# Scores and exponentials of the next batch moved ahead of product 1, and the softmax sums interleaved with the sums of r

## The chip, the cores and the metric

The kernel runs on one core of a Trainium2 chip. The metric is the device time of one launch in microseconds (us), the median of several executions. Before the change it is 144.81 us (three runs, 144.69 to 145.2). All times below come from one profiled execution of the same program, which took 144.88 us, and are counted from the start of its span.

## The reference

There are 8 batches. In each batch 8 heads hold x (512 x 64) and state (32 x 64). The first part is a cross attention in both directions, the second a two-branch layer with a maximum:

```python
scores  = scale * x @ state.T;  a  = softmax(scores)      # over the 32 states
xread   = a @ state                                        # 512 rows a head
scores2 = scale * state @ x.T;  a2 = softmax(scores2)      # over the 512 rows
sread   = a2 @ x                                           # 32 rows a head
rows    = concatenate([xread, sread])                      # 544 a batch, 512 wide
g       = maximum(rows @ w1, rows @ w2)                    # 1024 wide
out     = g @ w_out                                        # 4352 x 512, float32
```

The kernel uses max(h1, h2) = h2 + relu(h1 - h2), so that only one matrix, w1 - w2, needs a relu and the term h2 @ w_out goes through the product w2 @ w_out. It also puts the state through these matrices first, so that the attention weights a are multiplied with "state times weights".

## The kernel before

**Setup and pipeline.** A list of tokens at the head of the file (ORDER) writes out, instruction by instruction, the loading of the weights and the work of batches 0 and 1. Then a loop over b = 2 to 6 runs; each pass finishes batch b and prepares batch n = b + 1. A tail finishes batch 7 and the 256 sread rows. Nothing reorders the work: each engine executes its instructions in the order in which the code issues them, and engines wait for one another by semaphores.

**The pass of the loop.** The names that are used below:

- **l1** (line 375): eight banks f0 to f7 of PSUM get "state weights times a of b"; the relus go in turn to ACT (f0, f2, f4, f6, line 368) and DVE (f1, f3, f5, f7, line 370) and give r of the batch.
- **Seven products instead of eight** (line 426): r times w_out for 512 rows by 512 columns is made from seven quarter products, in Winograd's form of Strassen's scheme. Each is 8 matmuls of 256 columns. Three PSUM accumulators pX, pY and pZ take them. Their left sides are quarters of r (rq) or sums of those, st[0] to st[3], which DVE makes (**r_sum** 0 to 3, line 402, two bf16 inputs of 128 x 1024). r_sum 1 reads st[0], r_sum 3 reads st[1].
- **keep** 0, 1, 2 (line 102 on ACT) copies a partial accumulator away so that it can be added to a later one; **put** (line 402 or 104 on DVE, one on ACT) writes a quarter of the output; **opened** (line 432) adds the h2 term.
- For batch n: **sc_mm** (line 264, two halves of 8 small matmuls with xt, x transposed, as weights), **sc_ev** (line 272, an exponential on ACT for each half), **red** (lines 276 and 277, on DVE the sum over 32 states and its reciprocal, for each half), **mul** (line 280, on POOL the division of each half), **at_dma** (line 285, a transposing DMA of a on SP's queue), **sw_mm** (line 352, state times weights, three pairs of banks), **sw_ev** (their copies, mostly on ACT), **sr_mm** (line 304) and **sr_tr** (line 336) for sread.
- POOL further casts x of later batches (line 106) and makes differences of weights (line 402).

**Banks.** pX, pY and pZ have a bank each. The other five are used in a fixed ring: l1 takes eight turns of it, then sc_mm two, sw_mm five (one of its six banks is pY's), sr_mm one and sr_tr one or two. So the two banks of sc_mm are those of f3 and f4, and the last pair of sw_mm takes the banks of sc_mm.

**Buffers.** e, a and xt have two buffers each, used in turn by even and odd batches; the results of at_dma and the state weights sw have three.

Of the kernel before, what the change touches and what calls it, by code (L numbers as in the profile page):

```python
# [57 lines left out]
def kernel(  # L58
# [32 lines left out]
    def bank(ring="r", dtype=F32):  # L91
        if isinstance(ring, int):
            i = ring
        else:
            r = rings[ring]
            i = r[turn[ring] % len(r)]
            turn[ring] += 1
        return banks[i] if dtype == F32 else banks[i].bitcast(BF16)
# [142 lines left out]
    def xt_dma(b):  # L241
        nc.sync.dma_start_transpose(out=xt_s[b % 2].rearrange("p c k t -> p (c k) t"),
                                    in_=xb_s[b % 2].rearrange("p c m -> p (c m)"))
# [14 lines left out]
    def sc_mm(b, hh, ring="r"):  # L258
        p = bank(ring)
        pv = p.rearrange("p (c g i n) -> p c i g n", c=NC, g=2, i=2)  # L260
        for c in range(NC):
            for kk in range(2):
                k = 2 * hh + kk
                nc.tensor.matmul(pv[:, c, kk], xt_s[b % 2][:, c, k, :], sbd[:, b, k, :],  # L264
                                 start=(c == 0 and kk == 0), stop=(c == NC - 1 and kk == 1))
        return p

    def e_view(t, hh):
        return t.rearrange("p g c i n -> p (g c) i n")[:, :, 2 * hh:2 * hh + 2, :]

    def sc_ev(p, b, hh):
        nc.scalar.activation(out=e_view(e_s[b % 2], hh).rearrange("p (g c) i n -> p g c (i n)", g=2),  # L272
                             in_=p.rearrange("p (c g m) -> p g c m", c=NC, g=2), func=ACTF.Exp, scale=scale)

    def red(b, hh):
        nc.vector.tensor_reduce(es_all[:, b, hh], e_view(e_s[b % 2], hh), axis=AXX, op=ALU.add)  # L276
        nc.vector.reciprocal(er_s[b % 2][:, hh], es_all[:, b, hh])  # L277

    def mul(b, hh, eng):
        (nc.gpsimd if eng == "P" else nc.vector).tensor_mul(  # L280
            e_view(a_s[b % 2], hh), e_view(e_s[b % 2], hh),
            er_s[b % 2][:, hh].unsqueeze(3).to_broadcast([128, 2 * NC, 2, Ns]))

    def at_dma(b):
        nc.sync.dma_start_transpose(out=at_s[b % 3].rearrange("p g c t -> p (g c) t"),
                                    in_=a_s[b % 2].rearrange("p g c i n -> p (g c i n)"))
# [59 lines left out]
    def sw_mm(b, lo, hi, rA="r", rB="r"):  # L346
        pg = [bank(rA), bank(rB)]
        n = hi - lo
        for i in range(4):
            for g in range(2):  # L350
                rhs = wd[64 * g:64 * g + 64, i, lo:hi] if hi <= FF else wwo[64 * g:64 * g + 64, i, lo - FF:hi - FF]
                nc.tensor.matmul(pg[g][32 * i:32 * i + 32, 0:n],  # L352
                                 sbd[64 * g:64 * g + 64, b, i, 32 * g:32 * g + 32], rhs, start=True, stop=True)
        return pg

    def sw_ev(pg, b, lo, hi, g, eng):
        copy(eng, sw_s[b % 3][:, g, lo:hi], pg[g][:, 0:hi - lo])
# [14 lines left out]
    def l1_mm(b, f, ring="r"):  # L372
        p = bank(ring)
        for g in range(2):
            nc.tensor.matmul(p, sw_s[b % 3][:, g, f * 128:(f + 1) * 128], at_s[b % 3][:, g].rearrange("p c t -> p (c t)"),  # L375
                             start=(g == 0), stop=(g == 1))
        return p

    def l1_ev(p, b, f, eng=None):
        relu(r_s[b % 2][:, f, :], p, eng)  # L380
# [20 lines left out]
    def add(eng, o, i0, i1, op=ALU.add):  # L401
        (nc.gpsimd if eng == "P" else nc.vector).tensor_tensor(o, i0, i1, op=op)  # L402

    def wq(j, k):
        return wo[:, 4 * j:4 * j + 4, 256 * k:256 * k + 256]

    def rq(b, i, j):
        return r_s[b % 2][:, 4 * j:4 * j + 4, 256 * i:256 * i + 256]
# [5 lines left out]
    def r_sum(b, k, eng):  # L414
        a, c, op = ((rq(b, 1, 0), rq(b, 1, 1), ALU.add), (st[:, 0], rq(b, 0, 0), ALU.subtract),
                    (rq(b, 0, 0), rq(b, 1, 0), ALU.subtract), (rq(b, 0, 1), st[:, 1], ALU.subtract))[k]
        add(eng, st[:, k], a, c, op)
# [5 lines left out]
    def product(pv, lhs, rhs, first=False, cc=(0, 1)):  # L423
        for c in cc:
            for f in range(4):
                nc.tensor.matmul(pv[c], lhs[:, f, 128 * c:128 * c + 128], rhs[:, f, :],  # L426
                                 start=first and f == 0 and (c == 0 or pv.split), stop=False, skip_group_check=True)

    def opened(b, pv, i, rhs, cc=(0, 1)):
        for c in cc:  # L430
            for g in range(2):
                nc.tensor.matmul(pv[c], at_s[b % 3][:, g, 2 * i + c, :], rhs[:, g, :], start=False, stop=False,  # L432
                                 skip_group_check=True)
# [12 lines left out]
    def keep(k, pv, eng):  # L446
        if pv.split:
            for c in range(2):
                copy(eng[c], part[:, k, 256 * c:256 * c + 256], pv[c])
        else:  # L450
            copy(eng, part[:, k], pv.p[0])
# [11 lines left out]
    def so_half(b, k):  # L463
        return sw_s[b % 3][:, :, FF + 256 * k:FF + 256 * k + 256]

    def store(b, c0=0, c1=NC, lo=0, hi=DM, eng=None):
        dst = out[b * L:b * L + S].rearrange("(p c) n -> p c n", c=NC)
        (eng or nc.sync).dma_start(out=dst[:, c0:c1, lo:hi], in_=ob(b)[:, c0:c1, lo:hi])
# [265 lines left out]
    for b in range(2, B - 1):  # L734
        n = b + 1
        if b + 2 < B and b != 3:
            xt_dma(b + 2)
        for f in range(NF):
            l1_ev(l1_mm(b, f), b, f)
        pX, pY, pZ = Pair(BX), Pair(BY), Pair(BZ)  # L740
        product(pX, rq(b, 0, 0), wq(0, 0), True)
        keep(0, pX, "A")
        r_sum(b, 0, "V")
        r_sum(b, 1, "V")
        pp = [sc_mm(n, hh) for hh in range(2)]
        for hh in range(2):
            sc_ev(pp[hh], n, hh)
        product(pZ, rq(b, 0, 1), wq(1, 0), True)
        opened(b, pZ, 0, so_half(b, 0))
        pg = [sw_mm(n, 512 * z, 512 * z + 512, BY if z == 0 else "r") for z in range(3)]  # L750
        sw_ev(pg[0], n, 0, 512, 0, "A")
        sw_ev(pg[0], n, 0, 512, 1, "A")
        for hh in range(2):
            red(n, hh)
            mul(n, hh, "P")
        at_dma(n)
        if b == 3:
            xt_dma(b + 2)
        if b == 2:
            store(1)  # L760
        if b + 4 < B - 1:
            for g in range(2):
                load_x(b + 4, g)
        elif b + 4 < B:
            load_x(b + 4, 0, n=H)
        r_sum(b, 2, "V")
        product(pX, st[:, 1], wt[:, 1])
        sw_ev(pg[1], n, 512, 1024, 0, "A")
        keep(1, pX, "A")
        put(b, 0, 0, pZ, 0)  # L770
        sw_ev(pg[1], n, 512, 1024, 1, "V")
        sw_ev(pg[2], n, 1024, 1536, 0, "A")
        product(pY, st[:, 0], wt[:, 0], True)
        keep(2, pY, "A")
        r_sum(b, 3, "V")
        sw_ev(pg[2], n, 1024, 1536, 1, "A")
        if b + 2 < B:
            for k in range(4):
                cast_e(b + 2, k, "P")
        difference(n, "P")  # L780
        if b + 3 < B:
            for g in range(2):
                cast_b(b + 3, g, "P")
        if b < 6:
            v_sum(b - 2, "P")
        product(pX, st[:, 2], wt[:, 2])
        opened(b, pX, 1, so_half(b, 1))
        p = sr_mm(n, "r")
        put(b, 1, 1, pX, 2)
        sr_ev(p, n)  # L790
        if b < 4:
            sr_ev(srd[:, b - 2], b - 2)
        if n == B - 1:
            check_sums()
        product(pY, st[:, 3], wq(1, 1))
        opened(b, pY, 0, so_half(b, 1))
        put(b, 0, 1, pY, 1)
        product(pX, rq(b, 1, 1), wt[:, 3])
        opened(b, pX, 1, dif[:, b % 2])
        if b < 4:  # L800
            sr_cp(sr_tr(b - 2, "r"), b - 2, "A")
        sr_cp(sr_tr(n, "r"), n, "A")
        put(b, 1, 0, pX, None, "A")
        if n == B - 1:
            for k in range(4):
                m_sum(k, aq, sst, "P")
            p = bank("r")
            nc.tensor.matmul(p[:, 0:1], full, bad, start=True, stop=True)
            nc.vector.tensor_copy(flag[0:1, :], p[0:1, 0:1])
        store(b)  # L810
# [91 lines left out]
```

## Time and profile before

| What | Value |
|---|---|
| median of 3 runs | 144.81 us |
| the profiled execution | 144.88 us, its span 143.1 us |
| PE matmul busy | 134.7 us, 94% of the span |
| DVE / ACT / POOL busy | 108.3 / 86.9 / 72.1 us |
| the five passes of the loop | 52.72 to 119.47 us, 66.75 us |
| mean granted TensorE clock | 0.996 |

The view of stretches gives for each pass the busy time of every engine. The timeline lists an engine's instructions with start and duration; several of one kind in a row are one row with their count. The bracket behind a row is the idle time ahead of it and what ended it. The chain of waits follows the work that ended last backward; a row of it gives a start, a duration, an engine and a line.

### The profile page before, as it was taken

To read this page: it belongs to the slowest core of one execution; us is meant where nothing else is said; L and a number is where in the kernel's file an instruction comes from. 1 tells how busy PE (TensorE), PEld (TensorE's weight loads), DVE (VectorE), ACT (ScalarE), POOL (GpSimd) and SP (SyncE) were. 2 spreads that over 40 slices of the span, in tenths; PEclk is the share of its full clock that TensorE was granted. 3 is DMA by queue.
4 is the path that set the end of the run, shared out by engine and by line. 5 is a ranking of instruction groups with operands and counts; after the bars stand their busy time and mean duration, and the time that the engine had idled before them with its cause. 6 is when DMAs were issued, how large, how long until landed. Compare 5 with 4: busy or idle time off the path is not lost.

```text
span 143.1 us, 3680 instructions
## 1 busy us (share of the span) xinstructions
PE 134.7 (94%) x1448; PEld 95.4 (67%) x1458; DVE 108.3 (76%) x197; ACT 86.9 (61%) x168; POOL 72.1 (50%) x99
## 2 busy tenths in 40 slices
PE   6889989999999999999999999999999999999980
PEld 2467725456787776786778477747876786788860
DVE  3488959868999938997899799669948997847420
ACT  4367589895689535855682769086726855753220
POOL 4147326099009993399269908971990464200000
PEclk9999999999999999999999999999999999999998
DMA  3999999945997979949995999759137042502073
GB/s 112 342 366 392 384 386 386 343 83 93 196 343 230 286 180 249 236 42 293 242 386 109 212 355 195 160 213 211 35 65 293 2 58 82 234 5 73 9 248 119
DMA packets 36452, 29.50 MB, mean 206 GB/s; under 512 B 22608, under 2 KB 32336, under 8 KB 35536
## 3 DMA queue, kind: packets, MB, share of 16 engines
q1 hardware_dynamic: 36160, 29.10, 70.8%
q8 instruction: 12, 0.20, 0.6%
q10 hardware_dynamic: 272, 0.13, 0.3%
q14 instruction: 8, 0.07, 0.1%
HBM read 15.20 MB, written 8.91 MB: 169 GB/s over the span
## 4 chain that ended last, share of the span: by engine, by line
PE 83%; DMA 11%; ACT 1%; issue 1%; DVE 0%; SPq 0%; DVEq 0%
PE bank L426 36%; PE bank L375 19%; PE bank L432 10%; DMA big<-in_moe_w_out_dram 8%; PE bank L352 5%; DMA big<-in_x_dram 4%; PE bank L606 3%; PE bank L473 2%; PE bank L515 2%; PE bank L264 2%; PE bank L304 2%; PE bank L513 1%; ACT wo L102 1%; PE bank L548 1%; PE bank L336 0%
## 5 line engine op out<-in xcount | busy, mean ns | idle before, releaser
L102 ACT COPY big<-bank 128x512 f32<-128x512 f32 (+2 forms) x40 | 21.9, 551 | 16.6 <-PE bank L426 8.4
L280 POOL TENSOR_TENSOR a<-e,er 128x512 bf16<-128x512 bf16 x14 | 16.7, 1209 | 29.5 <-ACT e L272 18.0
L370 DVE TENSOR_SCALAR r<-bank 128x512 bf16<-128x512 f32 x32 | 21.9, 690 | 11.7 <-PE bank L375 10.6
L375 PE MATMUL bank<-at,sw 128*128 128x512 bf16 x120 | 29.1, 379 | 0.6 <-DVE sw L104 0.2
L426 PEld LDWEIGHTS <-big 128*128 128x128 bf16 x256 | 23.9, 98 | 6.3 <-DVE er L277 2.1
L426 PE MATMUL bank<-big,big 128*128 128x256 bf16 x192 | 23.1, 273 | 0.1
L102 ACT CAST sw<-bank 128x512 bf16<-128x512 f32 x36 | 20.1, 608 | 3.2 <-PE bank L352 3.2
L375 PEld LDWEIGHTS <-sw 128*128 128x128 bf16 x128 | 12.2, 98 | 13.5 <-ACT sw L102 0.5
L368 ACT ACTIVATE r<-bank 128x512 bf16<-128x512 f32 x32 | 18.3, 597 | 4.9 <-PE bank L375 4.7
L426 PEld LDWEIGHTS <-r 128*128 128x128 bf16 x192 | 18.2, 98 | 3.8 <-issue 0.5
L402 DVE TENSOR_TENSOR big<-bank,big 128x512 f32<-128x512 f32 (+1 forms) x25 | 16.4, 660 | 5.4 <-PE bank L432 5.4
L106 POOL CAST xe<-big 128x512 bf16<-128x512 f32 x23 | 16.5, 749 | 6.1 <-DMA big<-in_x_dram 6.1
L426 PE MATMUL bank<-wo,r 128*128 128x256 bf16 x128 | 16.3, 273 | 0.0
L102 ACT COPY sread_t<-bank 128x128 bf16<-128x128 bf16 x8 | 3.2, 472 | 18.7 <-PE bank L336 15.5
L106 POOL CAST xb<-big 128x1024 bf16<-128x1024 f32 x12 | 12.2, 1035 | 4.7 <-DMA big<-in_x_dram 4.7
L432 PE MATMUL bank<-sw,at 128*128 128x256 bf16 x96 | 14.4, 273 | 0.0
L432 PEld LDWEIGHTS <-at 128*128 128x128 bf16 x128 | 12.5, 98 | 1.7
L402 DVE TENSOR_TENSOR big<-r 128x1024 bf16<-128x1024 bf16 x16 | 12.6, 788 | 0.6
L276 DVE TENSOR_REDUCE sums<-e 128x16 f32<-128x512 bf16 x16 | 10.6, 660 | 0.3 <-ACT e L272 0.2
L272 ACT ACTIVATE e<-bank 128x512 bf16<-128x512 f32 x16 | 8.9, 601 | 1.3 <-PE bank L264 1.3
L402 POOL TENSOR_TENSOR big<-sw 128x512 bf16<-128x512 bf16 x8 | 9.2, 1151 | 0.9 <-POOL a L280 0.9
L104 DVE CAST sw<-bank 128x512 bf16<-128x512 f32 x12 | 7.9, 679 | 0.6 <-PE bank L352 0.6
(100 smaller groups left out, 188.7 us busy)
## 6 DMA issues: line engine op xcount, KB each, us to landing
big<-in_x_dram SPq DMA_DIRECT2D x14, 512.0 KB, 6.2
out_dram<-big SPq DMA_DIRECT2D x7, 1024.0 KB, 5.3
big<-in_moe_w_dram SPq DMA_DIRECT2D x8, 512.0 KB, 12.0
big<-in_moe_w_out_dram SPq DMA_DIRECT2D x4, 512.0 KB, 11.6
big<-in_x_dram SPq DMA_DIRECT2D x1, 1024.0 KB, 6.9
out_dram<-big SPq DMA_DIRECT2D x4, 256.0 KB, 2.6
sf<-in_state_dram SPq DMA_DIRECT2D x1, 384.0 KB, 10.4
out_dram<-w2m SPq DMA_DIRECT2D x2, 128.0 KB, 2.5
```

Source lines behind the costliest of these rows:

```text
L102: nc.scalar.copy(o, i)
L104: nc.vector.tensor_copy(o, i)
L106: nc.gpsimd.tensor_copy(o, i)
L272: nc.scalar.activation(out=e_view(e_s[b % 2], hh).rearrange("p (g c) i n -> p g c (i n)", g=2), in_=p.rearrange("p (c g m) -> p g c m", c= ...
L276: nc.vector.tensor_reduce(es_all[:, b, hh], e_view(e_s[b % 2], hh), axis=AXX, op=ALU.add)
L280: (nc.gpsimd if eng == "P" else nc.vector).tensor_mul(e_view(a_s[b % 2], hh), e_view(e_s[b % 2], hh), er_s[b % 2][:, hh].unsqueeze(3).to_b ...
L368: nc.scalar.activation(out=o, in_=p, func=ACTF.Relu)
L370: nc.vector.tensor_scalar(o, p, scalar1=0.0, scalar2=None, op0=ALU.max)
L375: nc.tensor.matmul(p, sw_s[b % 3][:, g, f * 128:(f + 1) * 128], at_s[b % 3][:, g].rearrange("p c t -> p (c t)"), start=(g == 0), stop=(g = ...
L402: (nc.gpsimd if eng == "P" else nc.vector).tensor_tensor(o, i0, i1, op=op)
L426: nc.tensor.matmul(pv[c], lhs[:, f, 128 * c:128 * c + 128], rhs[:, f, :], start=first and f == 0 and (c == 0 or pv.split), stop=False, ski ...
L432: nc.tensor.matmul(pv[c], at_s[b % 3][:, g, 2 * i + c, :], rhs[:, g, :], start=False, stop=False, skip_group_check=True)
```

## The change

It affects the loop alone, so five passes. In each pass the sixteen matmuls of sc_mm and the two exponentials stand directly behind l1, ahead of product 1 (pX) and keep 0. The sums of softmax, red, were issued for both halves after r_sum 1; now the first half stands between r_sum 0 and r_sum 1, and its mul is issued there as well. No instruction is added or taken away.

```diff
         for f in range(NF):
             l1_ev(l1_mm(b, f), b, f)
         pX, pY, pZ = Pair(BX), Pair(BY), Pair(BZ)
+        pp = [sc_mm(n, hh) for hh in range(2)]
+        for hh in range(2):
+            sc_ev(pp[hh], n, hh)
         product(pX, rq(b, 0, 0), wq(0, 0), True)
         keep(0, pX, "A")
         r_sum(b, 0, "V")
+        red(n, 0)
+        mul(n, 0, "P")
         r_sum(b, 1, "V")
-        pp = [sc_mm(n, hh) for hh in range(2)]
-        for hh in range(2):
-            sc_ev(pp[hh], n, hh)
         product(pZ, rq(b, 0, 1), wq(1, 0), True)
         opened(b, pZ, 0, so_half(b, 0))
         pg = [sw_mm(n, 512 * z, 512 * z + 512, BY if z == 0 else "r") for z in range(3)]
         sw_ev(pg[0], n, 0, 512, 0, "A")
         sw_ev(pg[0], n, 0, 512, 1, "A")
-        for hh in range(2):
-            red(n, hh)
-            mul(n, hh, "P")
+        red(n, 1)
+        mul(n, 1, "P")
         at_dma(n)
```

On DVE, in the pass of b = 2, behind the relu of f7 (L370); L402 are r_sum 0 and r_sum 1, L276 and L277 the sum and the reciprocal of a half:

```order
 L370 TENSOR_SCALAR r_105<-bank_65 128x512
 L402 TENSOR_TENSOR big_114<-r_105 128x1024
+L276 TENSOR_REDUCE sums_79<-e_92 128x16
+L277 RECIPROCAL er_96<-sums_79 128x16
 L402 TENSOR_TENSOR big_114<-big_114,r_105 128x1024
-L276 TENSOR_REDUCE sums_79<-e_92 128x16
-L277 RECIPROCAL er_96<-sums_79 128x16
 L276 TENSOR_REDUCE sums_79<-e_92 128x16
 L277 RECIPROCAL er_96<-sums_79 128x16
```

r_sum 1 has moved behind the first half's sum and reciprocal; the second half's pair stands where it stood.

On ACT, in the same pass, behind the relus of f4 and f6 (L368); the copy from bank_67 is keep 0, L272 are the exponentials, the casts are the first copies of sw:

```order
 L368 ACTIVATE r_105<-bank_66 128x512
 L368 ACTIVATE r_105<-bank_69 128x512
-L102 COPY big_115<-bank_67 128x512
 L272 ACTIVATE e_92<-bank_68 128x8x64
 L272 ACTIVATE e_92<-bank_66 128x8x64
+L102 COPY big_115<-bank_67 128x512
 L102 CAST sw_102<-bank_70 128x512
 L102 CAST sw_102<-bank_64 128x512
```

keep 0 has moved behind both exponentials. On PE the sixteen matmuls of sc_mm change places with the eight of product 1. The rows of POOL and of SP's queue stand in the same order as before.

## The prediction

> **What bounds the kernel now.** I read the page's busy times and chain first, then the stretches of the five passes (two of them and the sum are shown), then the chain and each engine's timeline within the pass of b = 3.
>
> ```profile
> span 143.1 us, 3680 instructions
> PE 83%; DMA 11%; ACT 1%; issue 1%; DVE 0%; SPq 0%; DVEq 0%
> 66.16:79.64 13.48, 13.42 (x162) 9.49 (x162) 11.90 (x23) 8.43 (x18) 9.37 (x11) 1.00 0.88 249
> 106.25:119.47 13.22, 13.17 (x162) 9.56 (x162) 11.35 (x22) 8.18 (x16) 4.57 (x4) 1.00 0.35 101
> sum 66.75, PE 66.46 PEld 47.58 DVE 56.22 ACT 41.20 POOL 41.56; mean PE 13.29 PEld 9.52 DVE 11.24 ACT 8.24 POOL 8.31
> ```
>
> In the loop PE is busy for 66.46 of 66.75 us at the full granted clock (1.00). An edit that adds and removes no PE work can therefore win only waits that hide inside PE's rows. The chain in the pass of b = 3 shows them:
>
> ```profile
> 66.43 3.19 PE bank L375 x14
> 69.61 0.87 PE bank L426 x8
> 70.48 0.47 PE bank L264 x16
> 70.95 0.87 PE bank L426 x8
> ...
> 73.03 2.77 PE bank L426 x24
> ...
> 76.60 0.01 issue
> 76.61 1.05 PE bank L426 x8
> ...
> 116.69 0.98 PE bank L426 x8
> ```
>
> A product takes 0.87; behind the narrow tiles of sw_mm or sr_mm its first matmul adds 0.11 (0.98 in the last pass). Three products would be 3 x 0.87 + 0.11 = 2.72; the row has 2.77, so some 0.05 are a wait. The product with st[3] takes 1.05 where 0.98 is enough: 0.07 more. Who is late there stands in the rows of the other engines:
>
> ```profile
> 69.65 0.69 DVE L370 TENSOR_SCALAR r<-bank 128x512 bf16<-128x512 f32 x1 [0.17 <-PE bank L375]
> 70.44 0.69 DVE L402 TENSOR_TENSOR big<-r 128x1024 bf16<-128x1024 bf16 x1
> 71.17 0.69 DVE L402 TENSOR_TENSOR big<-big,r 128x1024 bf16<-128x1024 bf16 x1
> 71.78 0.68 DVE L276 TENSOR_REDUCE sums<-e 128x16 f32<-128x512 bf16 x1
> 72.56 0.25 DVE L277 RECIPROCAL er<-sums 128x16 f32<-128x16 f32 x1
> 72.73 0.63 DVE L276 TENSOR_REDUCE sums<-e 128x16 f32<-128x512 bf16 x1
> 73.46 0.25 DVE L277 RECIPROCAL er<-sums 128x16 f32<-128x16 f32 x1
> 73.63 0.91 DVE L402 TENSOR_TENSOR big<-r 128x1024 bf16<-128x1024 bf16 x1
> 75.67 0.89 DVE L402 TENSOR_TENSOR big<-r,big 128x1024 bf16<-128x1024 bf16 x1
> 72.96 2.56 PEld L426 LDWEIGHTS <-big 128*128 128x128 bf16 x24 [0.42 <-DVE er L277]
> 74.11 0.61 ACT L102 COPY big<-bank 128x512 f32<-128x512 f32 x1
> 79.36 0.11 PEld L336 LDWEIGHTS <-sr 128*128 128x128 bf16 x2 [0.24 <-DVE sr L312]
> ...
> 79.40 0.24 PE bank L336 x2
> 92.89 0.06 PE bank L336
> ```
>
> r_sum 3 ends at 75.67 + 0.89 = 76.56 and its product starts at 76.61: it sets that start, and from DVE's end to PE's start lie 0.05. keep 1 ends at 74.11 + 0.61 = 74.72: it sets the third of the three products. The sr transposes wait for DVE for at most 0.24 in the first two passes, which have two of them; from the third on the one takes 0.06. The row at 72.96 names a reciprocal, but the product there reads st[1], which was ready at 71.17 + 0.69 = 71.86; what PE finishes ahead of it, the narrow tiles of sw_mm, sets 72.96. So the pass is PE's own work, and DVE's run of sums is the one neighbour that touches it.
>
> **The scores and exponentials.** The sixteen small matmuls take 0.47 on either side of product 1, and both ends of the pair stay: product 2 (pZ) starts where it did. They start 0.87 earlier, where product 1 started, and need the banks of f3 and f4 and xt of n:
>
> ```profile
> 67.20 1.75 ACT L368 ACTIVATE r<-bank 128x512 bf16<-128x512 f32 x3
> 68.00 1.48 DVE L370 TENSOR_SCALAR r<-bank 128x512 bf16<-128x512 f32 x2 [0.24 <-PE bank L375]
> 69.22 0.60 ACT L368 ACTIVATE r<-bank 128x512 bf16<-128x512 f32 x1 [0.27 <-PE bank L375]
> 69.45 1.04 PE L426 MATMUL bank<-wo,r 128*128 128x256 bf16 x8
> 70.58 0.59 ACT L102 COPY big<-bank 128x512 f32<-128x512 f32 x1 [0.76 <-PE bank L426]
> 71.06 1.09 ACT L272 ACTIVATE e<-bank 128x512 bf16<-128x512 f32 x2
> ```
>
> f4 is out at 67.20 + 1.75 = 68.95 and f3, the first of the DVE pair, half a pair in, at about 68.74; the scores come at 69.45. Margin 0.5. For xt the first pass is the tightest:
>
> ```profile
> 50.73 2.70 SPq L242 DMA_TRANSPOSE xt<-xb  x1
> xt<-xb SPq DMA_TRANSPOSE x1, 4.2
> 56.89 0.63 PE L264 MATMUL bank<-sbd,xt 128*128 128x64 bf16 x16
> ```
>
> It lands at 50.73 + 4.2 = 54.93; the scores move from 56.89 to 56.02. Margin 1.1. Cost of the move on PE: 0. Without that cover each 0.1 of lateness would cost 0.1 a pass.
>
> On ACT the relu of f6 ends at 69.22 + 0.60 = 69.82. The first half of the scores is done half of 0.47 and a matmul's drain behind 69.45, at about 69.9. The exponentials then run from about 69.9 to 71.0 (1.09), against 71.06 to 72.15 now. keep 0 goes 0.47 later with its product, from 70.58 to 71.05, and ends at 71.64. Its first reader is the new wait of the product with st[1] at 72.96: margin 1.3. The first copy of sw waits for PE's sw_mm, whose place doesn't move, so ACT and keep 1 stay where they are. Cost 0. The banks for the last pair of sw_mm come free 1.1 earlier; PE doesn't wait for them now, so that wins 0.
>
> **The sums on DVE.** This is where the change can touch the path. The steps, start to start, from the rows above: an instruction that needs nothing of the one ahead follows a two-input sum after 0.61 (71.17 to 71.78); reciprocal behind its sum 0.78 or 0.73; the next behind a reciprocal 0.17; r_sum 1 behind r_sum 0, whose result it reads, 0.73. Now r_sum 0 to r_sum 2 is 0.73 + 0.61 + 0.78 + 0.17 + 0.73 + 0.17 = 3.19 (70.44 to 73.63). After: 0.61 + 0.78 + 0.17 + 0.61 + 0.73 + 0.17 = 3.07, because r_sum 1 no longer stands directly behind the sum it reads. The first red starts at 71.05; its exponential is over at 70.5.
>
> But r_sum 1 then meets POOL:
>
> ```profile
> 72.95 2.50 POOL L280 TENSOR_TENSOR a<-e,er 128x512 bf16<-128x512 bf16 x2 [4.11 <-ACT e L272]
> 115.75 0.68 DVE L402 TENSOR_TENSOR big<-r,big 128x1024 bf16<-128x1024 bf16 x1
> ```
>
> The same kind of sum took 0.68 in the last pass, where POOL is idle, and 0.91 and 0.89 here with POOL busy: up to 0.23 more. mul starts 0.39 behind the start of its reciprocal (72.56 to 72.95), so at 71.83 + 0.39 = 72.22, while r_sum 1 runs from 72.00. Bounds: it ends at 72.69 untouched and at 72.92 in full contention. About two thirds of it overlap, so I take 0.15: end at 72.84, seen by PE at 72.89. The product wants it at 72.96. The margin falls from 1.1 to 0.07, and at the upper bound to nothing (72.97). If r_sum 1 came later still, keep 1 would take the first 0.05 and r_sum 3 the next 0.07, since PE waits for these anyway.
>
> r_sum 2 starts at 73.51 to 73.74, taken 73.66, against 73.63. Behind it the second mul starts 0.22 after r_sum 2 does (0.39 less 0.17), at 73.88; the first ended at 72.22 + 1.25 = 73.47. So r_sum 2 has 0.22 free of POOL and ends at about 73.66 + 0.84 = 74.50 instead of 74.54, ahead of keep 1's 74.72. r_sum 3 follows at a fixed distance: 0.04 earlier by this sum, 0.12 earlier to 0.11 later by the bounds. It gates PE in the first four passes, by 0.07 or less: -0.3 to +0.4 us for the whole run. I take 0.
>
> A rule speaks against this. The Trainium skill, "SBUF — State Buffer", section "Who interferes with whom", says that a VectorE instruction with two SBUF inputs and a GpSimd one that reads SBUF exclude each other: whichever starts first holds the port for its whole length. By it r_sum 2 at 73.63, with POOL's first mul running to 74.20, would now end at 74.89; it ended at 74.54, so this trace shows a slowing and not the full block. By the rule the changed r_sum 1, first by 0.22, would hold POOL back and end at 72.69; the mul would run to 73.94, r_sum 2 would end at 74.63, and the run would be up to 0.4 longer.
>
> **POOL and SP.** The second mul starts at 73.88 instead of 74.20 and ends 0.3 earlier, and so does the issue of the transposing DMA:
>
> ```profile
> 75.48 1.24 SPq L285 DMA_TRANSPOSE at<-a  x1
> at<-a SPq DMA_TRANSPOSE x6, 3.3
> ```
>
> It would land at about 78.5 instead of 75.48 + 3.3 = 78.8. Its reader is l1 of the next pass at 79.64, which doesn't wait for it. What lies behind it on SP's queue (xt's transposes, loads and stores) moves by at most these 0.3. Worth 0.
>
> The sum: 5 passes x (0 for PE, 0 for ACT, 0 for at) and 0 (-0.3 to +0.4) for r_sum 3. The span stays 143.1, the profiled execution 144.9, which stands 0.07 above the median. **Forecast 144.8**, own range 144.4 to 145.3. Changes under 0.5% (0.72 us) can't be told from none.
>
> **Rivals.**
> 1. DVE's run gets shorter by more than I take, and all visible waits vanish. For it: r_sum 1 loses its wait on r_sum 0. The ceiling is 5 x 0.05 (keep 1) + 4 x 0.07 (r_sum 3) + 2 x 0.24 (sr) = 1.0 us, so 143.8. Against it: keep 1 hangs on ACT and on sw_mm, which don't move, and the second part is worth 0.3. Between 143.8 and 144.4.
> 2. Slower: POOL's mul holds r_sum 1 for its whole length instead of slowing it. For it: they now start 0.22 apart, and what little r_sum 1 has left is 0.07. Held until the mul ends, it runs from 73.47 to 74.16, and PE waits until 74.21 instead of 72.96: 1.25 a pass, 6 us in all, 151. It decides once r_sum 1 takes over 1.0 us; a stretch to 1.2 would cost some 0.15 a pass, 145.6. The page named above has this as its rule where POOL is first. Against it: at 73.63 the same pair of instructions met with POOL first, and it cost 0.23.
> 3. A new wait on PE for what the scores need (bank, xt) or on keep 0: margins 0.5, 1.1 and 1.3. If the first were wrong by 0.3 beyond its margin, 1.5 us: 146.3.
> 4. The order changes but the lead of a is worth something, because l1 does wait for it. Against it: DVE, ACT and SP show no such wait, and the landing has 0.8 to spare.
>
> **The chances.** Forecast 0.80; rival 1 0.08 (half of it over the 0.5%); rival 2 0.08 (nearly all in its partial form); rival 3 0.03; rival 4 0.01, on the fast side. The range reaches from the upper part of rival 1 to the partial form of rival 2: 144.2 to 145.6. Faster by over 0.5%: 0.06; within: 0.84; slower: 0.10.
>
> **What would show it.** Right: passes of 13.2 to 13.5 us; the reciprocal of the first half starting 1.4 behind r_sum 0 and r_sum 1 0.17 behind that; the weights of st[1] still loaded about 3.5 behind the first matmul of line 264 (72.96 less 69.45); at_dma 0.3 earlier and no shorter pass. Wrong: a row of r_sum 1 of over 1.0 us, a wait of PE on the r_sum of st[1] or on line 264, or the row with 1.05 turning to 0.98 in every pass and the loop under 66.2 us.

## The result and the profile after

| | before | after |
|---|---|---|
| median, 12 runs each | 145.04 us | 145.94 us |
| profiled execution | 144.88 us | 145.69 us |
| its span | 143.1 us | 143.9 us |

The ratio is 1.007, with a 95% interval of 1.0051 to 1.0089. The change costs 0.9 us. The forecast was 144.8 us and no change, with a range up to 145.6. It started from 144.81, the median of three runs; over twelve runs the kernel before has 145.04, so 0.23 of the distance lies in the starting point and the rest in the change.

The stretches of the five passes after the change (pass, its length, then busy time and count of PE, PEld, DVE, ACT and POOL, granted clock, DMA share, GB/s):

```profile
52.63:66.57 13.94, 13.46 (x164) 9.50 (x162) 11.95 (x22) 8.09 (x16) 10.12 (x12) 1.00 0.90 217
66.57:80.61 14.04, 13.45 (x163) 9.51 (x162) 12.18 (x23) 8.53 (x18) 9.50 (x11) 1.00 0.81 226
80.61:93.83 13.22, 13.22 (x163) 9.53 (x161) 10.43 (x20) 8.51 (x17) 8.68 (x10) 1.00 0.91 219
93.83:107.06 13.23, 13.23 (x163) 9.53 (x161) 10.17 (x19) 8.28 (x16) 9.50 (x11) 1.00 0.64 142
107.06:120.29 13.23, 13.23 (x164) 9.56 (x162) 10.95 (x22) 8.28 (x16) 4.32 (x4) 1.00 0.39 101
sum 67.66, PE 66.59 PEld 47.64 DVE 55.68 ACT 41.69 POOL 42.13; mean PE 13.32 PEld 9.53 DVE 11.14 ACT 8.34 POOL 8.43
```

The loop takes 67.66 us instead of 66.75, and this 0.91 is the whole result. It isn't spread evenly. Against the passes before, 13.44, 13.48, 13.31, 13.30 and 13.22, the first two are 0.50 and 0.56 longer and the third and fourth 0.09 and 0.07 shorter. In the first two passes PE is also idle, for 0.48 and 0.59 (before, 0.05 and 0.06). So the question is what only the first two passes have: the sread rows of batches 0 and 1, whose normalisation (sr_ev on srd, which lies in the tile wz) and whose transpose are done there.

The chain of waits after the change, at the end of the pass of b = 3, with one row of the pass of b = 5 at the bottom (start, duration, engine and line; ... marks rows left out):

```profile
76.22 0.45 PE bank L432 x4
...
76.86 0.69 DVE big L402
77.55 0.09 DVE sums L310
...
77.66 0.48 DVE sr L312 x2
78.14 0.08 DVE sums L310
...
78.24 2.04 DVE sr L312 x2
...
80.33 0.28 PE bank L336 x2
80.61 3.45 PE bank L375 x16
...
104.28 0.98 PE bank L426 x8
```

Before, this chain ran on PE through the whole pass. Now it leaves PE for DVE: a put, then the sr_ev of n (0.48 for its two scalings), then the two scalings of the early sread row, 2.04, and only then the transpose on PE. The last row is the good news: the product with st[3] in the pass of b = 5 takes 0.98 and no longer 1.05.

Why 2.04 for two scalings of 128 x 64? The timelines of DVE and POOL, before (a row with x2 is the pair, and the x1 row with the same start its first half):

```profile
77.85 0.34 DVE L312 TENSOR_SCALAR sr<-wz,sums 128x64 bf16<-128x64 f32 x1
77.85 1.46 DVE L312 TENSOR_SCALAR sr<-wz,sums 128x64 bf16<-128x64 f32 x2
77.53 0.61 POOL L106 CAST xe<-big 128x512 bf16<-128x512 f32 x1
78.11 1.15 POOL L402 TENSOR_TENSOR big<-sw 128x512 bf16<-128x512 bf16 x1
```

and after, with the same scaling from PSUM (sr from bank) for comparison:

```profile
77.86 0.28 DVE L312 TENSOR_SCALAR sr<-bank,sums 128x64 bf16<-128x64 f32 x1
78.05 0.15 DVE L310 RECIPROCAL sums<-wz 128x2 f32<-128x2 f32 x1
78.24 1.05 DVE L312 TENSOR_SCALAR sr<-wz,sums 128x64 bf16<-128x64 f32 x1
78.24 2.03 DVE L312 TENSOR_SCALAR sr<-wz,sums 128x64 bf16<-128x64 f32 x2
78.09 1.15 POOL L402 TENSOR_TENSOR big<-sw 128x512 bf16<-128x512 bf16 x1
79.19 1.03 POOL L106 CAST xb<-big 128x1024 bf16<-128x1024 f32 x1
```

A scaling that reads PSUM takes 0.28. One that reads SBUF ends about 0.05 behind the POOL instruction that was running. Before, the first scaling came at 77.85, during a short cast of xe that ended at 78.14, and was over at 78.19; only the second met the difference (78.11 to 79.26). After, the difference starts at 78.09 and the first scaling at 78.24. So the first waits for the difference, ends at 79.29, and the second meets the cast of xb at 79.19. The pair was held by one long POOL instruction and is now held by two. The held time stands in the duration of the held instruction, not in an idle column, so the page showed DVE busy.

What moved? The pass of b = 3 begins 0.41 later in this execution. The scalings moved with it (77.85 to 78.24). POOL's difference did not (78.11 to 78.09): within the pass POOL is 0.43 ahead, and that is just the lead the interleaved sums gave it, for the second mul also ends 0.43 earlier in its pass (75.45 before, 75.43 after). DVE had won a lead too: r_sum 3 starts at 75.64, 0.44 earlier in the pass. But the put behind it has to wait for PE's matmuls of line 432, and there DVE's lead is lost:

```profile
76.86 0.69 DVE L402 TENSOR_TENSOR big<-bank,big 128x512 f32<-128x512 f32 x1 [0.32 <-PE bank L432]
```

The pass of b = 2, which starts at nearly the same time in both (52.72 and 52.63), shows the same swap: before, the first scaling starts at 64.36 and the difference at 64.62; after, the difference at 64.05 and the scaling at 64.20.

### The profile page after: what moved, and what is told of

The parts are those of the page before. It is cut to its first block, busy times and chain, and to the rows that moved or that the text cites. A ratio compares the mean times of both kernels' runs of the same rounds, so it can differ in the third digit from the quotient of the medians.

```text
span 143.9 us, 3693 instructions
## 1 busy us (share of the span) xinstructions
PE 134.9 (94%) x1458; PEld 95.3 (66%) x1458; DVE 107.9 (75%) x197; ACT 87.3 (61%) x168; POOL 73.0 (51%) x99
## 4 chain that ended last, share of the span: by engine, by line
PE 78%; DMA 11%; DVE 5%; ACT 1%; issue 1%; SPq 0%; DVEq 0%
PE bank L426 33%; PE bank L375 19%; PE bank L432 9%; DMA big<-in_moe_w_out_dram 8%; PE bank L352 5%; DVE sr L312 3%; DMA big<-in_x_dram 3%; PE bank L606 3%; PE bank L473 2%; PE bank L515 2%; PE bank L264 2%; PE bank L513 1%; PE bank L304 1%; DVE big L402 1%; ACT wo L102 1%; PE bank L548 1%
## 5 line engine op out<-in xcount | busy, mean ns | idle before, releaser
L280 POOL TENSOR_TENSOR a<-e,er 128x512 bf16<-128x512 bf16 x14 | 17.3, 1235 | 29.3 <-ACT big L102 17.8
L370 DVE TENSOR_SCALAR r<-bank 128x512 bf16<-128x512 f32 x32 | 21.9, 690 | 11.8 <-PE bank L375 11.4
L402 DVE TENSOR_TENSOR big<-bank,big 128x512 f32<-128x512 f32 (+1 forms) x25 | 16.5, 662 | 7.0 <-PE bank L432 6.5
L368 ACT ACTIVATE r<-bank 128x512 bf16<-128x512 f32 x32 | 18.3, 598 | 4.9 <-PE bank L375 4.7
L426 PE MATMUL bank<-wo,r 128*128 128x256 bf16 x128 | 15.5, 273 | 0.0
L402 DVE TENSOR_TENSOR big<-r 128x1024 bf16<-128x1024 bf16 x16 | 11.1, 697 | 0.6
L276 DVE TENSOR_REDUCE sums<-e 128x16 f32<-128x512 bf16 x16 | 10.8, 675 | 0.4 <-ACT e L272 0.4
L272 ACT ACTIVATE e<-bank 128x512 bf16<-128x512 f32 x16 | 8.9, 596 | 1.9 <-PE bank L264 1.3
L402 POOL TENSOR_TENSOR big<-sw 128x512 bf16<-128x512 bf16 x8 | 9.2, 1149 | 1.3 <-issue 1.3
```

Source lines behind the costliest of these rows:

```text
L280: (nc.gpsimd if eng == "P" else nc.vector).tensor_mul(e_view(a_s[b % 2], hh), e_view(e_s[b % 2], hh), er_s[b % 2][:, hh].unsqueeze(3).to_b ...
L368: nc.scalar.activation(out=o, in_=p, func=ACTF.Relu)
L370: nc.vector.tensor_scalar(o, p, scalar1=0.0, scalar2=None, op0=ALU.max)
```

## The experiments

Each is compared with the kernel before on the same chip; its median was 144.93 us beside e1 to e4 (23 runs) and 144.98 us beside e5 to e7 (29 runs). Most experiments have 12 runs, e2 has 8 and e4 has 6. The loop's length is from the profiled execution; the setup ahead of the loop varies by up to 0.8 us from one profiled execution to the next (the loop began between 52.63 and 53.41), so spans alone are not compared.

| Run | median us | ratio (95%) | loop us |
|---|---|---|---|
| before (first profile) | 145.04 | 1 | 66.75 |
| after | 145.94 | 1.007 (1.0051 to 1.0089) | 67.66 |
| e1 POOL later | 145.18 | 1.0015 (1.0005 to 1.0026) | 66.92 |
| e2 scalings on ACT | 144.47 | 0.9954 (0.9939 to 0.9969) | 66.23 |
| e3 scores alone | 145.24 | 1.0018 (1.0005 to 1.0032) | 67.01 |
| e4 sums alone | 146.50 | 1.0097 (1.0080 to 1.0115) | 67.98 |
| e5 before, scalings on ACT | 144.87 | 0.9991 (0.9971 to 1.0011) | 66.50 |
| e6 scalings earlier | 144.50 | 0.9967 (0.9950 to 0.9984) | 66.24 |
| e7 transpose later | 144.54 | 0.9975 (0.9953 to 0.9996) | 66.24 |

The theory is POOL's lead: the change lets POOL's long instructions start ahead of the two scalings, which are then held one after the other (below, a collision is a scaling held by such a long instruction). The rivals: the moved scores and exponentials cost the time themselves; DVE's own order or amount of work costs it, whatever POOL does; the late DVE costs it through other readers than the transpose.

### e1: POOL's lead taken away

The tile spare is new, 288 bf16 numbers in each partition; the line that makes it is left out here.

```diff
         sw_ev(pg[2], n, 1024, 1536, 1, "A")
+        if b < 4:
+            for _ in range(3):
+                nc.gpsimd.memset(spare, 0.0)
         if b + 2 < B:
```

> The changed kernel with about 1 us of POOL memsets of a spare tile behind the second mul, in the first two passes alone. Theory (POOL's lead): the change lost 0.50 and 0.56 us in the first two passes because POOL's difference and first cast of xb now start 0.3 to 0.6 ahead of the two scalings of the early sread rows on DVE (line 312 reading SBUF), which are held by POOL's instructions one after the other. With POOL 1 us later those scalings fall between the short casts again: passes of 13.3 to 13.5 instead of 13.94 and 14.04, 144.6 to 145.0 us, ratio to the kernel before 0.997 to 1.001. Rival (the moved scores and exponentials, or DVE's own order, cost the time, whatever POOL does): ratio stays at 1.007.

Measured 1.0015, just above the theory's 0.997 to 1.001 and far from the rival's 1.007.

```profile
52.67:66.25 13.58, 13.46 (x164) 9.50 (x162) 11.38 (x22) 8.10 (x16) 9.64 (x14) 1.00 0.89 204
66.25:79.91 13.66, 13.45 (x163) 9.50 (x162) 11.59 (x23) 8.53 (x18) 9.98 (x14) 1.00 0.90 246
```

```profile
L312 DVE TENSOR_SCALAR sr<-wz,sums x4: 541/868/1199, 64.2 to 78.4; 128x64 bf16<-128x64 f32 x4
```

The first two passes are 0.36 and 0.38 shorter than after the change, by nothing but idle work on POOL. They are not down to 13.4, and the scalings' durations (least, median, most, in ns) say why: the delay brought the first scaling back into the short casts (541 ns at the least) but left the second behind the difference (up to 1199), as before the change. The three memsets took 1.12, but the casts behind them took 2.28 instead of 2.74, so that the difference started only 0.61 later in the pass of b = 2 (12.03 behind its start, not 11.42). The size was missed, the mechanism is the expected one.

### e2: the scalings on ACT

```diff
-    def sr_ev(p, b):
+    def sr_ev(p, b, eng="V"):
         nc.vector.reciprocal(rr_all[:, b], p[:, 0:130:129])
         for g in range(2):
+            if eng == "A":
+                nc.scalar.mul(sr_s[b % 2][:, g, :], p[:, 1 + 64 * g:65 + 64 * g], rr_all[:, b, g:g + 1])
+                continue
...
-            sr_ev(srd[:, b - 2], b - 2)
+            sr_ev(srd[:, b - 2], b - 2, "A")
```

> The changed kernel with those four scalings (two in each of the first two passes) on ACT instead of DVE. Theory (POOL's lead): ACT is idle there and does not meet POOL, so the wait is gone altogether, the kernel before had some of it too: all passes 13.2 to 13.3, loop 66.2 to 66.4 against 66.75 before, 144.3 to 144.6 us, ratio 0.995 to 0.998. Rival: ratio stays at 1.007, since the loss is elsewhere.

Measured 0.9954: faster than both kernels. The first two passes take 13.28 each.

```profile
L313 ACT ACTIVATE sr<-wz,sums x4: 332/340/348, 65.0 to 78.6; 128x64 bf16<-128x64 f32 x4
sum 66.23, PE 66.23 PEld 47.76 DVE 51.84 ACT 42.87 POOL 42.13; mean PE 13.25 PEld 9.55 DVE 10.37 ACT 8.57 POOL 8.43
```

On ACT the same scaling of the same SBUF tile takes 332 to 348 ns in all four cases, beside a busy POOL. PE has no idle time left in the loop (66.23 of 66.23).

### e3: the scores and exponentials alone

```diff
         r_sum(b, 0, "V")
-        red(n, 0)
-        mul(n, 0, "P")
         r_sum(b, 1, "V")
...
-        red(n, 1)
-        mul(n, 1, "P")
+        for hh in range(2):
+            red(n, hh)
+            mul(n, hh, "P")
         at_dma(n)
```

> One part of the change alone: scores and exponentials ahead of product 1, the softmax sums behind r_sum 1 as before. Theory (POOL's lead): the first sum starts no earlier than before (71.8 in the pass of b = 3), POOL keeps its place, nothing is lost: 144.8 to 145.2 us, ratio 0.998 to 1.002. Rival (the moved scores and exponentials cost the time): 1.007.

Measured 1.0018, within the expected 0.998 to 1.002: the moved scores do not cost the 0.7%. The first two passes took 13.44 and 13.49, as before the change. Its interval stays just clear of 1. In its profile the chain of waits goes once through the transposing DMA of a, which landed 4.0 after its issue where 3.3 is the median; l1 of b = 6 stood behind it and took 3.61 where 3.45 is usual:

```profile
66.14:79.63 13.49, 13.48 (x163) 9.49 (x162) 11.92 (x23) 8.53 (x18) 9.39 (x11) 1.00 0.85 240
102.25 4.02 DMA at<-a
106.28 0.04 issue
106.32 3.61 PE bank L375 x16
```

The pass before it and its own came to 13.39 each, 0.09 and 0.17 more than before, and that is the whole 0.26 by which this loop is longer. Whether it accounts for the small excess of the timed runs too isn't settled; one execution shows it.

### e4: the interleaved sums alone

```diff
-        pp = [sc_mm(n, hh) for hh in range(2)]
-        for hh in range(2):
-            sc_ev(pp[hh], n, hh)
         product(pX, rq(b, 0, 0), wq(0, 0), True)
         keep(0, pX, "A")
+        pp = [sc_mm(n, hh) for hh in range(2)]
+        for hh in range(2):
+            sc_ev(pp[hh], n, hh)
```

> The other part alone: the sums interleaved with r_sum 0 and 1, scores and exponentials behind product 1 as before. Theory: the first sum waits for its exponential until 71.8, r_sum 1 starts at 72.7 and ends at about 73.4, so the product with st[1] waits on PE some 0.4 in each pass, and PE's delay leaves POOL ahead of it in the first two passes as well: 146.5 to 147.5 us, ratio 1.010 to 1.017. Rival (the interleaving is the harmless part, the scores the costly one): 1.000.

Measured 1.0097, just under the lower end, 1.010. DVE and PEld in the pass of b = 3:

```profile
72.17 0.69 DVE L276 TENSOR_REDUCE sums<-e 128x16 f32<-128x512 bf16 x1 [0.56 <-ACT e L272]
72.96 0.25 DVE L277 RECIPROCAL er<-sums 128x16 f32<-128x16 f32 x1
73.13 0.63 DVE L402 TENSOR_TENSOR big<-big,r 128x1024 bf16<-128x1024 bf16 x1
73.81 1.20 PEld L426 LDWEIGHTS <-big 128*128 128x128 bf16 x12 [0.80 <-DVE big L402]
107.49:121.06 13.57, 13.26 (x163) 9.55 (x162) 11.05 (x22) 8.28 (x16) 4.63 (x4) 1.00 0.35 98
```

The sum waits 0.56 for its exponential, r_sum 1 ends at 73.76 and the weights of st[1] load at 73.81. Even the last pass takes 13.57. So the two parts belong together: the early exponentials are what the interleaving needs. The second half of the expectation failed. PE's delay ahead of the scalings, 0.38 here (0.80 idle ahead of these weights, where it was 0.42), did not add a collision: POOL was late as well, the first scaling of the pass of b = 3 started at 78.65 and the difference at 78.81, and the pair took 1.35. The first two passes, 13.55 and 13.72, are no more than 0.15 off the others.

### e5: the kernel before, with the scalings on ACT

The edit of e2, made on the kernel before.

> The kernel before, with the scalings of the early sread rows on ACT instead of DVE. Theory (POOL's lead): this takes away the 0.12 that each of the first two passes lost at the sr transposes, and leaves the wait for r_sum 3 (0.08 in three passes): 144.6 to 144.8 us, ratio 0.997 to 0.999. If it comes to 0.995 like the changed kernel with the same edit, the change itself is worth nothing; the theory says that it is worth some 0.3 us once the collision is gone.

Measured 0.9991, a hair above the expected 0.999, with 1 inside the interval, so the timed runs alone show no gain. The profile has the size that was expected: the first two passes are 0.14 and 0.12 shorter, the loop 0.25.

```profile
53.13:66.43 13.30, 13.30 (x163) 9.56 (x162) 10.64 (x20) 8.58 (x18) 8.87 (x11) 1.00 0.81 198
66.43:79.79 13.36, 13.35 (x164) 9.59 (x162) 10.56 (x20) 9.02 (x20) 9.39 (x11) 1.00 0.89 250
```

The loop of e2 is another 0.27 us shorter (66.50 less 66.23): this is what the change itself is worth once the collision is gone. The medians, 144.87 and 144.47, come from two separate series and say the same with less certainty.

### e6: the scalings ahead of the put

```diff
+        if b < 4:
+            sr_ev(srd[:, b - 2], b - 2)
         put(b, 1, 1, pX, 2)
         sr_ev(p, n)
-        if b < 4:
-            sr_ev(srd[:, b - 2], b - 2)
```

> The changed kernel with those scalings still on DVE, but ahead of the put of quarter (1, 1), where DVE stood idle for 0.32 and POOL runs only the short casts of xe (0.61 each). Theory: each scaling waits for one short cast at most, the work of DVE that follows still ends ahead of the end of PE's pass: first two passes 13.2 to 13.5 instead of 13.94 and 14.04, ratio 0.996 to 0.999. Rival (what counts is DVE's amount of work there and not what POOL runs beside it): 1.005 to 1.007.

Measured 0.9967, as the theory has it. DVE does the same work on the same operands, at a place where POOL runs short casts beside it. The place also lets DVE use the 0.32 for which it stood idle, and the edit doesn't separate the two; the durations do, for a pair of scalings took 0.97 and not 2.03.

```profile
L312 DVE TENSOR_SCALAR sr<-wz,sums x4: 408/528/646, 63.3 to 77.0; 128x64 bf16<-128x64 f32 x4
66.58:79.86 13.28, 13.28 (x164) 9.58 (x162) 11.03 (x22) 8.53 (x18) 9.40 (x11) 1.00 0.86 237
```

A scaling takes 408 to 646 ns beside the casts of xe, where it took 1044 to 1058 after the change.

### e7: the transpose one pass later

```diff
+        if b in (3, 4):
+            sr_cp(sr_tr(b - 3, "r"), b - 3, "A")
         p = sr_mm(n, "r")
...
-        if b < 4:
-            sr_cp(sr_tr(b - 2, "r"), b - 2, "A")
         sr_cp(sr_tr(n, "r"), n, "A")
```

> The changed kernel with the scalings where they are, but their transpose on PE one pass later, so that PE does not stand behind them. Theory: DVE still loses about 1 us in each of the first two passes (the scalings take 1.05 each), but PE no longer waits for it at the pass's end; a rest may show at the relus of the next l1, whose first comes 0.3 later: loop 66.2 to 66.7, ratio 0.996 to 1.001. Rival (the late DVE costs the time through the put and the relus behind it, not through the transpose): 1.004 to 1.007.

Measured 0.9975, as the theory has it.

```profile
L312 DVE TENSOR_SCALAR sr<-wz,sums x4: 1042/1052/1060, 64.3 to 78.6; 128x64 bf16<-128x64 f32 x4
65.94:79.22 13.28, 13.28 (x164) 9.62 (x162) 12.07 (x23) 8.73 (x17) 9.45 (x11) 1.00 0.91 257
```

The scalings are held as long as after the change (1042 to 1060 ns), yet the pass takes 13.28. DVE's late put and relus cost nothing that shows; the loss reaches the end through the one transpose that PE has in front of the next l1.

## Why the prediction was wrong, step by step

**The bound.** Right for the last three passes, which are PE's own work and came to 13.22 and 13.23. In the first two the chain leaves PE for DVE at the end of the pass, and there the bound did not hold.

**The scores and exponentials.** Right: banks, xt and keep 0 held their margins, and e3 shows the move alone at 1.0018.

**DVE's run of sums.** The order of starts was right: the first reciprocal came 1.39 behind r_sum 0 (predicted 1.4), r_sum 1 0.17 behind it, and the weights of st[1] loaded 3.51 behind the first matmul of the scores (predicted 3.5). The stretch of r_sum 1 was not there:

```profile
72.42 0.63 DVE L402 TENSOR_TENSOR big<-big,r 128x1024 bf16<-128x1024 bf16 x1
72.63 1.31 POOL L280 TENSOR_TENSOR a<-e,er 128x512 bf16<-128x512 bf16 x1 [4.35 <-ACT big L102]
73.91 0.63 DVE L402 TENSOR_TENSOR big<-r 128x1024 bf16<-128x1024 bf16 x1
```

r_sum 1 took 0.63, not 0.84; the mul, which started second, took 1.31. Before, the first mul alone took 1.05:

```profile
72.95 1.05 POOL L280 TENSOR_TENSOR a<-e,er 128x512 bf16<-128x512 bf16 x1 [4.11 <-ACT e L272]
```

Here is the first wrong reading. I halved a merged row (2.50 for two) and let the first mul end at 74.20. It ended at 72.95 + 1.05 = 74.00, and r_sum 2, whose row ran from 73.63 to 74.54, ended 0.54 behind it, no more than the 0.63 that it takes undisturbed. r_sum 3 of the same pass ended at 76.56, 0.55 behind POOL's first cast, which ran from 75.40 to 76.01. So r_sum 2 had been held to the end of the mul, as the rule of the Trainium skill says ("SBUF — State Buffer", section "Who interferes with whom"). The trace agreed with the rule, and I rejected the rule because of a mean. The runs bear it out further: the scalings on DVE end with POOL's instruction, those on ACT don't. The same section of the Trainium skill counts tensor_scalar, which has one tensor input, among the operations that can take the shared port. The scalings from SBUF were held in this case; I had weighed only the two-input sums.

**The step that failed: "POOL and SP ... Worth 0".** I saw that POOL would run 0.3 ahead and asked only who waits for a. The lead was 0.43. I did not ask what POOL's later instructions would then meet on DVE. Neighbours that exclude each other make an earlier engine a changed neighbour. The row that carried the loss stood in the prediction: PE waiting 0.24 at the sr transposes. I used it as a ceiling of a gain, without asking who made DVE late there, and none of the signs of being wrong that I listed looks at these transposes. This wait became 0.76 and 0.86 in the two passes:

```profile
66.28 0.11 PEld L336 LDWEIGHTS <-sr 128*128 128x128 bf16 x2 [0.76 <-DVE sr L312]
80.32 0.11 PEld L336 LDWEIGHTS <-sr 128*128 128x128 bf16 x2 [0.86 <-DVE sr L312]
```

The sum of it: 0.52 and 0.62 more at the transposes, and 0.23 less at the product that r_sum 3 had delayed (by 0.02 in the first pass and 0.07 in each of the next three), 0.91 in all. The loop grew by 0.91.

**The gain.** Another term was mis-sized, in the change's favour. r_sum 3 was to start between 0.12 earlier and 0.11 later; it started 0.44 earlier in the pass, mostly because r_sum 2 met only the last 0.03 of the first mul and took 0.63 (0.91 before, 0.84 in the forecast). For the whole run this was to gain 0, and at best 0.3. Passes 3 and 4 won 0.09 and 0.07, and with the collision gone (e2 against e5) the loop won 0.27, in line with that best case.

**The rivals.** Rival 2 named the right mechanism, POOL excluding DVE, but at r_sum 1, where DVE comes first. The price fell on another pair. Rival 3 was not seen, and rival 4 only in the one late a of e3. Rival 1 was right that DVE's run gets shorter by more than I took. Its ceiling was 1.0; removing all the waits but keep 1's brought 66.23 against 66.75, so 0.52. The part for the transposes, 2 x 0.24, was too large: e5 took that wait away and won 0.25 (13.44 to 13.30 and 13.48 to 13.36, within rounding).

## What to carry to other kernels

When an edit lets an off-path engine run earlier, list what it will now run beside, above all where two engines exclude each other (here POOL against DVE's scalings from SBUF and its two-input sums); an earlier start can put a long instruction ahead of a short one that the path needs. A held instruction shows as a long one, not as idle time: compare an instruction's duration with its shortest twin (here 0.34 against 1.05) before believing that an engine is busy. Don't take the end of one instruction from the mean of a merged row.

Three versions of the change are 0.3 to 0.5% faster than the kernel before and can't be told apart: the two early scalings on an idle ACT (144.47 us, 0.9954 of before), the scalings on DVE beside shorter POOL work (144.50), and their reader one pass later (144.54). Their loops are 66.23, 66.24 and 66.24.

## What the hardware showed beyond the expected

A DVE scaling of 128 x 64 from SBUF took anything from 341 to 1198 ns in the kernel before, with the same shape and types, and ended about 0.05 us behind a POOL instruction all four times; from PSUM it took 273 to 285 ns:

```profile
L312 DVE TENSOR_SCALAR sr<-bank,sums x12: 273/280/285, 48.8 to 117.4; 128x64 bf16<-128x64 f32 x12
L312 DVE TENSOR_SCALAR sr<-wz,sums x4: 341/770/1198, 64.4 to 78.1; 128x64 bf16<-128x64 f32 x4
```

POOL was busy beside it in every run, so no row shows what it takes from SBUF with POOL idle. The shortest took 254 ns, in e4. DVE's other instructions that read SBUF were not all held: after the change a sum over 32 states started inside the first mul (72.63 to 73.94) and took 0.67, where it had taken 0.68 before with POOL idle (the row at 71.78 in the prediction).

```profile
72.96 0.67 DVE L276 TENSOR_REDUCE sums<-e 128x16 f32<-128x512 bf16 x1
```
